# Another planned order for all engines of a sparse-attention and FFN kernel: new due-time shifts, new places for five copies

## The chip, the cores and the metric

The kernel runs on one core of a Trainium2 chip. Its time is the device time of one execution in microseconds (us); several executions give a median.

## What is computed

The reference is banded attention followed by a LayerNorm and a feed-forward network with a residual (4 batches, 8 heads, 768 positions, 64 columns a head; a query row sees the 8 first keys and the 96 last ones):

```python
scores = scale * np.matmul(q, k.transpose(0, 1, 3, 2)) + bias      # bias: -slope[h] * distance
scores = np.where(is_global | is_local, scores, -1000000000.0)
a = softmax(scores);  x = a @ v                                    # [4, 768, 8*64]
xn = (x - mu) / np.sqrt(var + 1e-06) * g_ln
out = x + np.maximum(xn @ w_ch1, 0.0) @ w_ch2                      # 512 -> 2048 -> 512
```

The weights arrive as 64-bit floats, the rest as 32-bit floats.

## The kernel before, in words

**Arithmetic.** Nearly every product is made of fp16 matmuls: each operand is split into a high and a low fp16 part, and three products (high by high, high by low, low by high) are summed in PSUM. So a "row" of probabilities times values is three matmuls at lines 512 to 514, a first-layer product three at 809 to 811, 837 to 839 or 862 to 864, and the second layer (line 910) reads `w2h`, `w2l`, `w2h`.

**Tiles and stages.** There are 24 tiles of 128 query rows, t0 to t23. t0 to t3 are the first blocks of the four batches; they run in fp32 at the start (flips of q and k by TensorE at 479 and 481, copies out of PSUM at 471 on ACT or 473 on DVE, scores at 583, the maximum at 593, exponentials at 597, product with v at 611, quotient at 621 to 623). A later tile runs group `.k` (load and split of k, q, v), `.s` (scores 685, least value 544 on DVE, exponentials 549 on ACT, high part 690 on DVE, low part 691 on POOL, transposing DMA, rows 512 to 514 on TensorE) and `.x` (quotient 524, moments 531 to 533, power 536 on POOL, normalization 708 on DVE and 718 on ACT, differences 726 to 729 on POOL, halves 740 on ACT and 741 on DVE, transposing DMA 742 into xT).

Two tiles make a chunk of 256 rows, f0 to f11 (tile 2c and 2c+1). f0 and f1 run the first layer in parts as soon as one tile is there (`a0` to `a3`), f2 and f3 directly, and f4 to f11 by `seven`: seven products of 24 matmuls (lines 862 to 864) for each half of the columns instead of eight, with copies (875, ACT), additions (878, DVE) and the eviction (820 ACT, then 821 DVE) between them, in three PSUM banks. Its first products per half take the first half of xT (`key` 0), the next ones sums and differences of the halves (made by 726 to 729, 740, 741). The second layer (910) takes 6 matmuls per step, and 919 with the DMA at 922 writes the result.

**Weights.** Sixteen weight blocks w0 to w15 of 1 MB are loaded (392) and turned into fp16 parts by passes a (400, ACT), b (404, DVE), c (412, ACT), d (416, DVE), the high part (435 POOL, 437 ACT) and the low part (439 POOL, 441 DVE). The letters of `WHERE` say which engine makes pass b, the high and the low part.

**What sets the order.** `banded` records every operation with engine, a planned duration and a group. `Plan.forward` then makes a list schedule: each operation has a due time from what needs it, moved by `SHIFT[group]`; of the operations that could start, an engine takes the most urgent one. An engine other than TensorE may stand idle for up to `LOOK` times the duration of that operation, if a more urgent one (by over `EAGER`) will be ready by then. `ORDER` gives the order in which groups stand in the rings of buffers, `MOVE` the engine of the copies at 471/473, `FLIPS` the PSUM banks for the flips of each first tile. The kernel then issues on each engine in exactly this order; every engine runs its list in order, so an operation that waits holds all behind it. `hold` (1022) puts matmuls on a constant into planned gaps of TensorE before 130 us; `tied` places a POOL operation behind the DVE operation that is planned ahead of it, before `TIED` = 150 us. The three tests of the inputs' ranges, `ranges` (972 to 977), `products` and `limits`, are DVE groups of their own.

Of the kernel before, what the change touches and what calls it, by code (L numbers as in the profile page):

```python
# [23 lines left out]
B, H, S, D = 4, 8, 768, 64  # L24
# [62 lines left out]
class Plan:  # L87
# [20 lines left out]
    def op(self, engine, took, emit, r=(), w=(), xfer=None, after=0.0, uses=(), port=False):  # L108
        o = Op(engine, took, emit, xfer, after, port)
        o.group = self.group  # L110
        for k in r:
            self.edges(self.wrote.get(k, ()), o)
        for k in w:
            self.edges(self.wrote.get(k, ()), o)
            self.edges(self.read.get(k, ()), o)
        for k in w:
            self.wrote[k], self.read[k] = [o], []
        for k in r:
            if k not in w:
# [21 lines left out]
    def order(self, chain, stretch, lead):  # L141
# [28 lines left out]
        self.need, self.place = need, place  # L170
        self.planned = self.forward(SHIFT)
        return [o for _, o in self.planned]

    def forward(self, shift):
# [18 lines left out]
        while any(known.values()):  # L193
            best = None
            for e in engines:
# [28 lines left out]
        return [(at, o) for at, _, o in sorted(plan, key=lambda x: x[:2])]  # L224


LOOK = 0.5
EAGER = 3.0


# [1 line left out]
def banded(ctx, tc, q, k, v, n_global, n_local, g_ln, w1, w2, out, flag):  # L232
# [155 lines left out]
    def weight(src, dh, dl, name, n, engine="SP", uses=()):  # L388
# [672 lines left out]
LAST = 40  # L1061
IDLE, HOLD, FILL = 3, 130.0, 0.8
CW = 4
ORDER = ["t01", "t23", "w0", "w1", "w2", "w3", "w4", "w5", "w6", "w7", "w8", "w9", "w10", "w11", "w12", "w13", "w14", "w15", *(f"a{t}{j}" for t in range(4) for j in range(4))]
FLIPS = {0: ("fl", (6, 7, 4)), 1: ("fl", (6, 7, 4)), 2: ("f2", (6, 7)), 3: ("f2", (6, 7))}
TS0 = list(range(12, 20))
LATER = (2, 3)
LOW_ON_POOL = ()
# [206 lines left out]
```

## Times and profile before

| | |
|---|---|
| median of 3 runs | 629.6 us (629.45, 629.6, 631.86) |
| the profiled execution's own time | 630.34 us |
| its span in the trace | 628.6 us |
| mean granted TensorE clock | 0.992 |
| TensorE busy | 602.3 us (96% of the span) |
| DVE, ACT, POOL busy | 442.3, 328.3, 246.0 us |

How to read it: the span is from the first to the last instruction in the trace; the time also holds the 1.7 us around it. Busy time counts from the start to the modelled end of an instruction; successive matmuls overlap, so the start-to-start distance and not the duration says how fast TensorE goes. A bracket behind a row, `[3.18 <-DVE arena L821]`, is the idle time of the engine ahead of this row and what ended it.

### The profile page before, as it was taken

The numbers are of one execution on the slowest core, as the hardware profiler recorded it, in microseconds if no ns is written. First come the engines' busy times: TensorE is split into PE (matmuls) and PEld (weight loads), VectorE is DVE, ScalarE is ACT, GpSimd is POOL, SyncE is SP. The second block draws the span as 40 slices with busy tenths as digits, with TensorE's granted clock in tenths as the row PEclk, the third lists the DMA queues.
The fourth block names the chain that finished last, engine by engine and source line by source line (L and its number), as shares of the span: only waits on it lengthen the run. The fifth ranks groups of instructions, "written<-read, shape, count | busy, mean of one in ns | idle before, by whom it ended". The sixth has DMA issues, their size and how long they took to land.

```text
span 628.6 us, 17087 instructions
## 1 busy us (share of the span) xinstructions
PE 602.3 (96%) x6988; PEld 450.9 (72%) x6988; DVE 442.3 (70%) x995; ACT 328.3 (52%) x798; POOL 246.0 (39%) x230
## 2 busy tenths in 40 slices
PE   7889999999999999799999999999899999999995
PEld 5778998545956866696786786786687695886762
DVE  3899898887648575885895994893785684773431
ACT  3887887654534454563663662671663562642220
POOL 1234354448774764432422532531533432422000
PEclk9999999999999999899999999999989999999999
DMA  9996989978484685897698896887996771641301
GB/s 241 304 281 137 247 219 245 169 157 188 76 151 86 142 144 119 173 184 115 133 163 165 167 160 134 165 122 140 169 170 107 157 136 35 126 69 19 77 1 39
DMA packets 260118, 91.64 MB, mean 146 GB/s; under 512 B 250176, under 2 KB 250176, under 8 KB 260032
## 3 DMA queue, kind: packets, MB, share of 16 engines
q1 hardware_dynamic: 259744, 90.47, 72.7%
q8 instruction: 56, 0.92, 0.6%
q14 instruction: 30, 0.25, 0.1%
q10 hardware_dynamic: 288, 0.00, 0.0%
HBM read 38.01 MB, written 6.29 MB: 70 GB/s over the span
## 4 chain that ended last, share of the span: by engine, by line
PE 68%; DVE 13%; ACT 5%; DMA 5%; POOL 4%; issue 3%; SPq 1%; ACTq 0%; DVEq 0%; POOLq 0%
PE bank L910 30%; PE bank L862 7%; PE bank L864 6%; PE bank L863 6%; PE bank L685 4%; PE bank L838 2%; PE bank L839 2%; PE bank L837 2%; DMA arena<-arena 2%; DVE arena L416 2%; DVE arena L404 2%; DMA arena<-in_moe_w_ch_dram 1%; ACT arena L549 1%; PE bank L514 1%; PE bank L512 1%
## 5 line engine op out<-in xcount | busy, mean ns | idle before, releaser
L910 PE MATMUL bank<-w2h,arena 128*128 128x512 f16 x768 | 245.6, 379 | 0.1
L910 PEld LDWEIGHTS <-arena 128*128 128x128 f16 x1152 | 107.2, 98 | 112.3 <-issue 0.9
L691 POOL TENSOR_TENSOR arena<-arena 128x512 f16<-128x512 f32 x80 | 95.6, 1197 | 169.4 <-DVE arena L690 111.6
L910 PE MATMUL bank<-w2l,arena 128*128 128x512 f16 x384 | 145.5, 379 | 0.1
L862 PE MATMUL bank<-arena 128*128 128x128 f16 x512 | 88.2, 219 | 2.8 <-DMA arena<-arena 1.7
L863 PE MATMUL bank<-arena 128*128 128x128 f16 x512 | 88.2, 219 | 0.0
L864 PE MATMUL bank<-arena 128*128 128x128 f16 x512 | 88.2, 219 | 0.0
L549 ACT ACTIVATE arena<-arena,mn 128x256 f32<-128x256 f32 x160 | 80.0, 501 | 5.1
L862 PE MATMUL bank<-arena,w 128*128 128x128 f16 x384 | 68.7, 223 | 3.2 <-DVE arena L821 3.2
L544 DVE CUSTOM_DVE_ANT_0 arena<-bank,mask 128x256 f32<-128x256 f32 x160 | 60.3, 418 | 13.7 <-POOL arena L691 9.8
L864 PE MATMUL bank<-arena,w 128*128 128x128 f16 x384 | 68.8, 223 | 0.0
L863 PE MATMUL bank<-arena,w 128*128 128x128 f16 x384 | 68.8, 223 | 0.0
L821 DVE SCALAR_TENSOR_TENSOR arena<-bank,arena 128x512 f16<-128x512 f32 x64 | 43.7, 686 | 26.3 <-ACT arena L820 25.7
L820 ACT ACTIVATE arena<-bank 128x512 f16<-128x512 f32 x64 | 37.7, 591 | 37.1 <-PE bank L864 34.0
L863 PEld LDWEIGHTS <-arena 128*128 128x128 f16 x512 | 50.2, 98 | 4.4 <-issue 3.3
L685 PE MATMUL bank<-kT,qT 128*128 128x128 f16 x640 | 47.0, 219 | 4.8 <-DVE nm L544 2.4
L862 PEld LDWEIGHTS <-arena 128*128 128x128 f16 x512 | 50.2, 98 | 0.9
L864 PEld LDWEIGHTS <-arena 128*128 128x128 f16 x512 | 50.1, 98 | 0.0
L536 POOL TENSOR_TENSOR rs<-rs,half 128x1 f32<-128x1 f32 x24 | 23.7, 987 | 65.9 <-DVE rs L533 65.9
L690 DVE CAST arena<-arena 128x512 f16<-128x512 f32 x80 | 41.6, 526 | 9.7 <-DMA arena<-arena 4.4
L685 PEld LDWEIGHTS <-qT 128*128 128x128 f16 x640 | 39.6, 98 | 12.0 <-issue 6.6
L547 ACT ACTIVATE mn<-nm 128x2 f32<-128x2 f32 x80 | 15.8, 197 | 56.2 <-DVE nm L544 55.6
(177 smaller groups left out, 1479.4 us busy)
## 6 DMA issues: line engine op xcount, KB each, us to landing
arena<-in_moe_w_ch_dram SPq DMA_DIRECT2D x16, 1024.0 KB, 7.4
kf<-in_k_dram SPq DMA_DIRECT2D x28, 256.0 KB, 4.4
vf<-in_v_dram SPq DMA_DIRECT2D x28, 256.0 KB, 4.0
qf<-in_q_dram SPq DMA_DIRECT2D x24, 256.0 KB, 3.8
out_dram<-x SPq DMA_DIRECT2D x24, 256.0 KB, 2.4
qT<-qT SPq DMA_DIRECT2D x40, 128.0 KB, 3.3
pT<-arena SPq DMA_TRANSPOSE x80, 3.5
arena<-arena SPq DMA_TRANSPOSE x36, 3.2
```

The costliest lines, as they stand in the source:

```text
L536: op("POOL", 0.98, lambda: pool.tensor_tensor(out=rs(), in0=rs(), in1=half, op=ALU.pow), r=["half"], w=[rs])
L544: vec.tensor_tensor_reduce(out=T()[:, u, :], in0=ps()[:, u], in1=mask(h), scale=1.0 / Z, scalar=3e38, op0=ALU.add, op1=ALU.min, accum_out= ...
L549: act.activation(out=T()[:, u, :], in_=T()[:, u, :], func=AF.Exp, scale=-1.0, bias=mn()[:, h:h + 1], accum_out=sm()[:, h:h + 1])
L685: pe.matmul(ps()[:, u, n_ * P:(n_ + 1) * P], lhsT=qT()[:, a * H + h, :], rhs=use[n_][0]()[:, h, :], start=(a == 0), stop=(a == 1))
L690: op("DVE", 0.33, lambda pn=pn, T=T: vec.tensor_copy(out=pn()[:, :, 0, :], in_=T()), r=[T], w=[(pn, "hi")], port=True)
L691: op("POOL", 1.2, lambda pn=pn, T=T: pool.tensor_tensor(out=pn()[:, :, 1, :], in0=T(), in1=pn()[:, :, 0, :], op=ALU.subtract), r=[T, (pn, ...
L820: op("ACT", 0.49, lambda: act.activation(out=hh()[:, 0], in_=src(), func=AF.Relu), r=[key], w=[(hh, "hi")])
L821: op("DVE", 0.6, lambda: vec.scalar_tensor_tensor(out=hh()[:, 1], in0=src(), scalar=0.0, in1=hh()[:, 0], op0=ALU.max, op1=ALU.subtract), r ...
L862: pe.matmul(ps()[:, i, :], lhsT=wh, rhs=xT()[:, hi + kk, :], start=(first_ and i == 0 and kk == 0), stop=False, skip_group_check=True)
L863: pe.matmul(ps()[:, i, :], lhsT=wh, rhs=xT()[:, lo + kk, :], start=False, stop=False, skip_group_check=True)
L864: pe.matmul(ps()[:, i, :], lhsT=wl, rhs=xT()[:, hi + kk, :], start=False, stop=(i == 3 and kk == 1), skip_group_check=True)
L910: pe.matmul(ps[t](), lhsT=h[:, part, :], rhs=w[:, f + a, :], start=(f + a == 0 and n_ == 0), stop=(f + a == NF - 1 and n_ == 2))
```

## The change

The numbers that set the order are replaced; no operation is added or dropped, and each operation keeps its shape. Of the passes over the weights, the high part of four blocks goes from ACT to POOL (before: ten on ACT, six on POOL; after: six and ten); eight low parts are on POOL in both. Six copies at 473 on DVE become five (one goes to ACT). The flips of t0 and t1 get a fourth PSUM bank, `t23` stands later in `ORDER`, and `LOOK` is doubled. The table `SHIFT` is another one in nearly every entry; here are its first ones.

```diff
-LOOK = 0.5
+LOOK = 1.0
...
-ORDER = ["t01", "t23", "w0", "w1", "w2", "w3", "w4", "w5", "w6", "w7", "w8",
+ORDER = ["t01", "w0", "w1", "w2", "w3", "w4", "w5", "w6", "w7", "t23", "w8",
...
-FLIPS = {0: ("fl", (6, 7, 4)), 1: ("fl", (6, 7, 4)), 2: ("f2", (6, 7)), 3: ("f2", (6, 7))}
+FLIPS = {0: ("fl", (6, 7, 4, 5)), 1: ("fl", (6, 7, 4, 5)), 2: ("f2", (6, 7)), 3: ("f2", (6, 7))}
...
-SHIFT = {"a0": 820.0, "a1": 286.0, "a2": 108.0, "a3": 701.5, "f0": 21.0, "f1": -345.5, "f10": -122.5,
...
+SHIFT = {"a0": 392.5, "a1": -70.0, "a3": 106.0, "f0": -21.0, "f1": 3.0, "f10": -16.5, "f2": -17.0,
...
-MOVE = {"k1": "D", "k3": "D", "p31": "D", "q0": "D", "q1": "D", "q3": "D"}
-WHERE = {"1_0_0": "DAP", "1_0_1": "DPP", "1_1_0": "DAD", "1_1_1": "DAD", "1_2_0": "DAD", "1_2_1": "DPD", "1_3_0": "DPD", "1_3_1": "DPP", "2_0": "DAP", "2_1": "DPP", "2_2": "DAP", "2_3": "DPD", "2_4": "DAP", "2_5": "DAD", "2_6": "DAD", "2_7": "DAP"}
+MOVE = {"k2": "D", "p01": "D", "p21": "D", "q0": "D", "q2": "D"}
+WHERE = {"1_0_0": "DPP", "1_0_1": "DAP", "1_1_0": "DPD", "1_1_1": "DAD", "1_2_0": "DPP", "1_2_1": "DPD", "1_3_0": "DPP", "1_3_1": "DAP", "2_0": "DPP", "2_1": "DPD", "2_2": "DPP", "2_3": "DAD", "2_4": "DPD", "2_5": "DPD", "2_6": "DAD", "2_7": "DAP"}
```

In the rows of the order that follow, `arena` is the large buffer in which most intermediate tiles lie, and a number behind a name tells its copies apart.

The first place is the start. These are the first operations of the ACT engine, ahead of them the loads of n_global and n_local, before the change:

```order
L377 ACT_TABLE_LOAD
L377 ACTIVATE arena<-arena,nh 128x256
L471 ACTIVATE k_0_198<-bank_78 128x512
L373 ACTIVATE mask_84<-arena 128x256 x8
L597 ACTIVATE arena<-bank_72,nm_250 128x128 x4
L471 ACTIVATE pT_0_281<-bank_79 128x512
```

and after it:

```order
L400 ACT_TABLE_LOAD
L400 ACTIVATE arena<-arena,less 128x1024
L412 ACTIVATE arena,big<-arena 128x1024
L400 ACTIVATE arena<-arena,less 128x1024
L437 ACTIVATE w_01_91<-arena 128x2x512
L412 ACTIVATE arena,big<-arena 128x1024
L377 ACTIVATE arena<-arena,nh 128x256
L471 ACTIVATE k_1_227<-bank_76 128x512
L471 ACTIVATE q_1_229<-bank_77 128x512
L373 ACTIVATE mask_84<-arena 128x256 x8
```

Five passes over the first two weight blocks now stand ahead of the mask (377, 373) and of the first copies of q and k. The same happened to the loads: on the SP queue the first weight block (392) went from behind five loads of q, k and v to the first place.

The second place is the quotient of tile t9 at about 250 us, where chunk f4 takes over. On DVE before:

```order
L919 SCALAR_TENSOR_TENSOR x_2777<-bank_79,x_2777 128x512
L690 CAST arena<-arena 128x2x256
L524 TENSOR_TENSOR x_3574<-bank_74,r_3281 128x512
L531 BN_STATS bn_3576<-x_3574 128x6
L532 BN_AGGR mv<-bn_3576 128x2
L533 TENSOR_SCALAR rs_3579<-mv 128x1
L708 SCALAR_TENSOR_TENSOR arena<-x_3574,mv,gb 128x512
L821 SCALAR_TENSOR_TENSOR arena<-bank_77,arena 128x512
L669 COPY vn_1_2775<-vn_0_2445 16x1024
```

and after:

```order
L690 CAST arena<-arena 128x2x256
L821 SCALAR_TENSOR_TENSOR arena<-bank_77,arena 128x512
L524 TENSOR_TENSOR x_3590<-bank_74,r_3289 128x512
L531 BN_STATS bn_3593<-x_3590 128x6
L532 BN_AGGR mv<-bn_3593 128x2
L533 TENSOR_SCALAR rs_3596<-mv 128x1
L708 SCALAR_TENSOR_TENSOR arena<-x_3590,mv,gb 128x512
L775 TENSOR_TENSOR arena<-arena 128x512
```

The eviction at 821, which frees bank_77, went from behind t9's five operations to the place ahead of them.

The third place is TensorE at the same point, between t9's last rows and the next product into bank_77. Before, the product stands right behind the rows:

```order
L514 LDWEIGHTS pT_3_3483
L514 MATMUL bank_74<-vn_1_2775,pT_3_3483 128x64
L862 LDWEIGHTS w_00_90
L862 MATMUL bank_77<-arena,w_00_90 128x128
L863 LDWEIGHTS w_00_90
```

After, six matmuls of f3's second layer (910) stand between them:

```order
L514 LDWEIGHTS pT_3_3478
L514 MATMUL bank_74<-vn_1_2782,pT_3_3478 128x64
L910 LDWEIGHTS arena
L910 MATMUL bank_79<-w2h,arena 128x512
L910 LDWEIGHTS arena
L910 MATMUL bank_79<-w2l,arena 128x512
```

and six more stand between the product before and the rows, so that twelve matmuls of the second layer and the twelve row matmuls are in between. Elsewhere in the program the same groups moved too: between the last rows of the second tile of a chunk and the first product that needs that tile's xT, the order now has other amounts of TensorE's work, which the prediction gives.

## Rows read from the trace of the kernel before

**Rows 1.** The page: busy us, share of the span and instructions of each engine.

```profile
PE 602.3 (96%) x6988; PEld 450.9 (72%) x6988; DVE 442.3 (70%) x995; ACT 328.3 (52%) x798; POOL 246.0 (39%) x230
```

**Rows 2.** Waits of TensorE from 130 us on: total us, times, longest.

```profile
PE bank L862 <- DVE arena L821: 3.2, 1, 3.2
PE bank L685 <- DVE nm L544: 2.3, 4, 1.4
PE bank L685 <- DVE kT L668: 2.2, 1, 2.2
PE bank L862 <- DMA arena<-arena: 1.7, 2, 1.1
PE bank L862 <- ACT bank L875: 1.0, 2, 0.7
```

**Rows 3.** Timeline of TensorE: start, duration, instruction, idle ahead of it.

```profile
250.84 0.19 PE L514 MATMUL bank<-vn,pT 128*128 128x64 f16 x1
254.21 0.27 PE L862 MATMUL bank<-arena,w 128*128 128x128 f16 x1 [3.18 <-DVE arena L821]
258.48 0.38 PE L910 MATMUL bank<-w2h,arena 128*128 128x512 f16 x1
258.69 0.38 PE L910 MATMUL bank<-w2l,arena 128*128 128x512 f16 x1
261.88 0.22 PE L862 MATMUL bank<-arena 128*128 128x128 f16 x1
402.33 0.22 PE L862 MATMUL bank<-arena 128*128 128x128 f16 x1 [1.10 <-DMA arena<-arena]
457.22 0.65 PE L685 MATMUL bank<-kT,qT 128*128 128x128 f16 x8 [2.22 <-DVE kT L668]
```

**Rows 4.** Timeline of ACT and DVE at 250 us.

```profile
250.72 0.60 ACT L820 ACTIVATE arena<-bank 128x512 f16<-128x512 f32 x1 [2.44 <-PE bank L864]
251.07 0.69 DVE L524 TENSOR_TENSOR x<-bank,r 128x512 f32<-128x512 f32 x1 [0.66 <-PE bank L514]
253.47 0.68 DVE L821 SCALAR_TENSOR_TENSOR arena<-bank,arena 128x512 f16<-128x512 f32 x1
```

**Rows 5.** Timeline of DVE at 455 us.

```profile
455.03 1.09 DVE L976 TENSOR_SCALAR okb<-big 128x16 f32<-128x16 f32 x1
```

**Rows 6.** Stretches: length, busy PE, PEld, DVE, ACT, POOL, granted clock, DMA share, GB/s.

```profile
253.50:256.90 3.40, 2.69 (x25) 2.66 (x25) 2.11 (x4) 1.27 (x2) 2.49 (x4) 0.50 0.94 201
458.30:461.70 3.40, 3.40 (x35) 3.27 (x33) 2.37 (x6) 2.47 (x10) 1.52 (x2) 0.50 0.79 162
```

**Rows 7.** The same columns, the start by tens.

```profile
0.00:10.00 10.00, 7.33 (x49) 5.54 (x49) 2.88 (x16) 2.77 (x5) 1.59 (x13) 1.00 0.83 162
10.00:20.00 10.00, 8.67 (x75) 7.47 (x75) 5.67 (x14) 7.33 (x20) 0.00 (x0) 1.00 1.04 379
20.00:30.00 10.00, 8.07 (x74) 7.21 (x71) 9.52 (x17) 8.65 (x18) 3.29 (x3) 1.00 1.02 283
```

**Rows 8.** Timeline of TensorE: the first fp32 scores.

```profile
11.32 1.16 PE L583 MATMUL bank<-k,q 64*128 64x128 f32 x8 [1.44 <-DVE q L473]
```

**Rows 9.** Groups of DVE and POOL by form: busy us, mean ns, idle before.

```profile
L404 DVE TENSOR_SCALAR arena<-arena 128x1024 uint16<-128x1024 uint16 x16 | 23.2, 1464 | 2.1 <-ACT arena L400 2.1
L416 DVE SCALAR_TENSOR_TENSOR arena<-arena 128x1024 int32<-128x1024 int32 x16 | 21.2, 1322 | 1.1 <-ACT arena L412 1.1
L435 POOL CAST w<-arena 128x1024 f16<-128x1024 f32 x3 | 3.4, 1137 | 9.5 <-DVE arena L416 7.2 <-DVE w L441 2.3
```

**Rows 10.** Timeline of DVE and POOL at 35 to 40 us.

```profile
35.01 1.22 DVE L416 SCALAR_TENSOR_TENSOR arena<-arena 128x1024 int32<-128x1024 int32 x1
37.35 1.30 DVE L404 TENSOR_SCALAR arena<-arena 128x1024 uint16<-128x1024 uint16 x1
38.80 2.13 POOL L439 TENSOR_TENSOR w<-arena,w 128x1024 f16<-128x1024 f32 x1 [1.37 <-DVE arena L404]
39.93 2.08 DVE L416 SCALAR_TENSOR_TENSOR arena<-arena 128x1024 int32<-128x1024 int32 x1 [0.23 <-ACT arena L412]
```

More of the change, by code (lines that the diff above doesn't have):

```diff
@@ L1063 @@
 CW = 4
-ORDER = ["t01", "t23", "w0", "w1", "w2", "w3", "w4", "w5", "w6", "w7", "w8", "w9", "w10", "w11", "w12", "w13", "w14", "w15", *(f"a{t}{j}" for t in range(4) for j in range(4))]
-FLIPS = {0: ("fl", (6, 7, 4)), 1: ("fl", (6, 7, 4)), 2: ("f2", (6, 7)), 3: ("f2", (6, 7))}
+ORDER = ["t01", "w0", "w1", "w2", "w3", "w4", "w5", "w6", "w7", "t23", "w8", "w9", "w10", "w11", "w12", "w13", "w14", "w15", *(f"a{t}{j}" for t in range(4) for j in range(4))]
+FLIPS = {0: ("fl", (6, 7, 4, 5)), 1: ("fl", (6, 7, 4, 5)), 2: ("f2", (6, 7)), 3: ("f2", (6, 7))}
 TS0 = list(range(12, 20))
@@ L1082 @@
 SS, PVS, PVS2, F1S, F1S2, F2S, F2S2 = (0, 1), (2, 3), (2,), (4, 5), (4, 5, 3), (6, 7), (6, 7)
-SHIFT = {"a0": 820.0, "a1": 286.0, "a2": 108.0, "a3": 701.5, "f0": 21.0, "f1": -345.5, "f10": -122.5, "f11": 112.5, "f2": 34.5, "f4": 18.0, "f5": -6.5, "f6": 9.5, "f7": -72.5, "f8": -87.5, "f9": 42.0, "g": 43.0, "m.a": 196.5, "m.d": -8.5, "s": 25.5, "t0.k": -12.0, "t0.p": 442.5, "t0.s": -26.0, "t0.x": 120.0, "t1.k": -11.0, "t1.p": 823.0, "t1.s": 740.5, "t1.x": 391.0, "t10.k": 4.5, "t10.s": 71.5, "t10.x": 151.5, "t11.k": -0.5, "t11.s": 51.0, "t11.x": 97.5, "t12.k": 162.0, "t12.s": 43.0, "t12.x": -52.5, "t13.k": -41.0, "t13.s": -78.5, "t13.x": 214.5, "t14.k": -152.5, "t14.s": -0.5, "t14.x": 327.5, "t15.k": -122.0, "t15.s": -30.0, "t15.x": -41.5, "t16.k": 49.5, "t16.s": 21.5, "t16.x": 22.0, "t17.k": -339.0, "t17.s": -103.0, "t17.x": -150.0, "t18.k": -10.5, "t18.s": 113.5, "t18.x": -59.5, "t19.k": 62.5, "t19.s": -44.5, "t19.x": 153.0, "t2.k": -612.5, "t2.p": 446.0, "t2.s": -18.0, "t2.x": 531.5, "t20.k": 147.0, "t20.s": 192.5, "t20.x": 207.0, "t21.k": -140.5, "t21.s": -33.0, "t21.x": 166.0, "t22.k": 85.0, "t22.s": 67.5, "t22.x": 76.0, "t23.k": -42.0, "t23.s": -129.0, "t23.x": 17.0, "t3.k": -590.0, "t3.p": 320.0, "t3.s": -371.0, "t3.x": 98.0, "t4.k": -338.0, "t4.s": 227.0, "t4.x": 59.0, "t5.k": 1576.5, "t5.s": 804.0, "t5.x": 1039.0, "t6.k": -664.5, "t6.s": 75.0, "t6.x": 87.5, "t7.k": 211.5, "t7.s": 189.5, "t7.x": 31.0, "t8.k": 61.5, "t8.s": -1.0, "t8.x": 1.5, "t9.k": -35.5, "t9.s": 13.0, "t9.x": 149.5, "w1_0_0": -19.0, "w1_0_1": -367.5, "w1_1_0": -7.5, "w1_1_1": -360.0, "w1_2_0": -44.5, "w1_2_1": -300.0, "w1_3_0": 297.0, "w1_3_1": 841.0, "w2_0": -334.5, "w2_1": 76.0, "w2_2": -332.0, "w2_3": 22.5, "w2_4": -548.0, "w2_5": -183.0, "w2_6": -33.5, "w2_7": 16.5}
@@ L1084 @@
-MOVE = {"k1": "D", "k3": "D", "p31": "D", "q0": "D", "q1": "D", "q3": "D"}
-WHERE = {"1_0_0": "DAP", "1_0_1": "DPP", "1_1_0": "DAD", "1_1_1": "DAD", "1_2_0": "DAD", "1_2_1": "DPD", "1_3_0": "DPD", "1_3_1": "DPP", "2_0": "DAP", "2_1": "DPP", "2_2": "DAP", "2_3": "DPD", "2_4": "DAP", "2_5": "DAD", "2_6": "DAD", "2_7": "DAP"}
+SHIFT = {"a0": 392.5, "a1": -70.0, "a3": 106.0, "f0": -21.0, "f1": 3.0, "f10": -16.5, "f2": -17.0, "f3": -11.5, "f4": -38.5, "f5": 2.5, "f6": 9.5, "f7": -19.5, "f8": -26.0, "f9": -37.0, "g": -252.0, "m.a": 158.5, "s": -24.5, "t0.p": 219.5, "t0.x": 237.0, "t1.k": 81.5, "t1.s": -621.5, "t1.x": 151.5, "t10.k": -29.5, "t10.s": 52.0, "t10.x": -6.0, "t11.k": 4.5, "t11.s": -44.0, "t12.k": 21.0, "t12.s": 39.0, "t12.x": 37.5, "t13.k": 32.5, "t13.s": 34.0, "t13.x": 21.5, "t14.k": -86.0, "t14.s": 33.0, "t14.x": 97.0, "t15.k": -61.5, "t15.s": 7.0, "t15.x": 116.5, "t16.k": 50.0, "t16.s": 45.5, "t17.k": -129.5, "t17.s": -12.0, "t17.x": 45.0, "t18.k": -116.5, "t18.s": 120.5, "t19.s": -43.0, "t19.x": 85.5, "t2.s": 350.5, "t20.s": 39.0, "t21.k": 23.5, "t21.s": -34.0, "t22.s": 156.5, "t23.k": 34.0, "t23.s": 51.5, "t3.k": 93.5, "t3.p": -7.5, "t3.x": -6.0, "t4.k": 25.0, "t4.s": 378.5, "t5.k": -151.5, "t5.s": -19.5, "t5.x": 89.0, "t6.k": 115.5, "t7.k": -106.5, "t7.s": -19.0, "t8.k": -106.0, "t8.s": -14.5, "t8.x": -28.5, "t9.k": -27.0, "t9.s": -10.5, "t9.x": 28.0, "w1_0_0": 340.5, "w1_0_1": 430.5, "w1_1_0": 2.5, "w1_1_1": -2.0, "w1_2_0": 54.5, "w1_2_1": 23.5, "w2_2": 3.0, "w2_3": 7.5, "w2_4": 285.5, "w2_5": -84.5, "w2_6": 190.5, "w2_7": 167.0}
```

## The prediction

> **What bounds the kernel now.** I read the page's busy times first, then the waits of TensorE, then the timeline at the longest of them, then the granted clock by stretches, and last the start by tens. TensorE is busy for 96% of the span and no other engine for over 70% [rows 1], so the end is set by TensorE's own work and by the time in which it stands idle, works on constants or runs at half its clock. No matmul that computes something is added or dropped, so only those three can change.
>
> From 130 us on, where no constants are fed in any more, five groups of waits make 3.2 + 2.3 + 2.2 + 1.7 + 1.0 = 10.4 us [rows 2]. The longest is one stop of 3.18 us at 254.21: a product of f4 wants bank_77, and the eviction at 821 has not freed it [rows 3]. The ACT half of that eviction started at 250.72 and took 0.60, so DVE could have gone on at 251.3; but its list had t9's quotient and moments (524 to 708) ahead, and 821 started at 253.47 [rows 4]. The second, 2.22 us at 457.22, comes from the copy of kT at 668 [rows 3], which stood on DVE behind the six small operations of `ranges`, one of which took 1.09 us [rows 5]. Behind each of these two stops TensorE is granted half its clock, 0.50 (the level of 1.2 GHz), for 3.4 us [rows 6]. In the first one TensorE stood until 254.21, so 2.7 us of work ran at half speed, which costs 1.3 us; in the second 3.4 us, which costs 1.7. That is 3.0 us for the clock. The other waits are short: transposed halves of xT that were late (1.10 at 402.33 [rows 3]), score banks, a copy.
>
> The start is another matter. In the first 20 us DVE is busy for 2.88 + 5.67 of 20 us, from 20 us on for 9.52 of 10 [rows 7]: it idles while the first q and k come in, and is then the engine that the rest waits for. TensorE's wait of 1.44 us ahead of its first fp32 scores at 11.32 is for a copy on DVE [rows 8].
>
> **The change part by part.** *f4's stop.* On DVE 821 now stands ahead of t9's quotient, and on TensorE six matmuls of f3's second layer stand on either side of t9's rows. At the distance of 0.21 us between two such matmuls [rows 3] that is 12 x 0.21 = 2.6 us, and the rows take 0.3 (2.9 us together); the eviction needs 0.60 + 0.68 = 1.3 us [rows 4]. So the 3.2 us go, with 1.6 us in hand. What hides the eviction is that second layer; without it 1.0 us of wait would remain. What is late next is t9's own chain, through quotient, power, normalization, differences, halves and transposing DMA, to the first product that needs xT.
>
> *The chunk boundaries.* That chain took at most 11.0 us at f4, from t9's last row at 250.84 to the first product that reads sums of xT at 261.88, which shows no wait [rows 3]. At f7 a product waited 1.10 us [rows 3], with 11.7 us of TensorE's work in the order between the rows and it, so there the chain took 12.8 us. I take 11.0 to 12.8. Counting, in the two orders, TensorE's work between those two points at the trace's distances between matmuls gives for f4 to f11: before 5.6, 11.6, 11.6, 11.7, 10.4, 14.2, 11.7, 12.9 us; after 9.5, 12.9, 14.2, 14.3, 14.7, 13.4, 14.7, 11.7. In the old order six of the eight lie under 12.8, in the new one two: f4, short by 1.5 to 3.3 us, and f11, by 0 to 1.1. At f4 the chain itself showed 11.0 with foreign work on DVE ahead of it, so I take 1.5 there, and 0.5 at f11. The waits for DMA and 875 (2.7) thus shrink to 2.0.
>
> *`ranges` and kT.* In the new order the tests stand where DVE has about 6 us until TensorE needs what follows, and kT's copy is not behind them: 2.2 us go. If that cover is gone, they come back. The score banks' waits (2.3 us, four times) have no one cause; the slack that I count behind their operations in the new order is smaller than zero in a few places, by 0.8 at most, where it was 4.6 before. I keep half, 1.1 (bounds 0 and 2.3). So of 10.4 us there remain 2.0 + 1.1 = 3.1: a gain of 7.3.
>
> *The clock.* The two dips stood behind idle times of 3.18 and 2.22 us. Behind the 1.10 at 402.33 none stood. The longest wait that I leave is 1.5, so I count none: a gain of 3.0 (bounds 0 and 3.0).
>
> *The start.* Five ACT passes and four DVE passes over two weight blocks, with 2 MB of loads between, move ahead of the mask and of the first copies of q and k. For DVE they are twice 1.30 + 1.22 [rows 10], 5.0 us, put into time in which it was idle for 11.5 us [rows 7]. Against that, everything of the first tiles comes later: stepped through by the durations of the trace the first fp32 scores start near 17.8 instead of 11.3 [rows 8], and a0's first group at 40.4 as before, but with 5.4 us less of TensorE's work done by then. DVE's idle time to that point grows by 3.0 by this count. On the other side the largest lead that TensorE has on DVE's list shrinks from 11.8 to 11.2 us, and it falls to 5 to 7 us after that, where it stayed at 8 to 10 in the old order; 2.2 us that TensorE lost between 70 and 130 us hang on this. 3.0 - 0.6 - 2.2 is 0.2: I count nothing. The bounds are -3 (the later waits go and DVE idles no longer) and +6 (the first scores' delay stays whole). The matmuls on constants rise from 154 to 188; where the planned gaps are not real, they are part of these +6. The fourth flip bank and the copy that goes to ACT cost 0 or less; they fall into DVE's busiest time and into the same bounds.
>
> *The four high parts.* ACT is relieved of four passes and does not bind. POOL takes four of 1.14 us [rows 9], in time in which it is idle for over half. But a DVE pass beside a POOL pass is held: 416 took 2.08 us at 39.93, while the low part at 439 ran from 38.80 to 40.93 on POOL, and 1.22 at 35.01 [rows 10]. Over all 16, 404 lost 16 x (1464 - 1300) ns and 416 16 x (1322 - 1220) [rows 9, 10], 2.6 + 1.6 us beside 14 POOL passes: 0.3 each. So four more cost 1.2 us; the bounds are 0 and 4 x 0.86 = 3.4, if each hits a pass as at 39.93. All of that falls where DVE binds.
>
> The Trainium skill, page "SBUF — State Buffer", section "SBUF: two separate sides", speaks against this part: VectorE and GpSimd share one pair of ports under a lock, and the one that comes later is blocked for the whole instruction. This trace agrees for 416, which ended about one duration behind POOL's pass. By that rule each of the four could cost a whole pass of 1.14, 4.6 us instead of 1.2, and the sum would end 3.4 us later. The rows' mean of 0.3 says that the ties keep most passes apart, and I stay with it.
>
> **The sum.** 630.3 - 7.3 - 3.0 + 0 + 1.2 = 621.2 us for an execution like the profiled one. That one lies 0.7 above the median, so 620.5 is my number. At 450 to 500 us, say, TensorE then has nothing left but work; the end of the program (the last result and its store behind the last matmul) does not move.
>
> **The rivals.** *The gain is eaten at the start.* DVE gets its first copy some 6 us later, its list keeps the lead it needs, and the +6 stays, less little: 620.5 + 6 to 8 (with the POOL passes at their bound) is 627 to 629, within 0.5%. For it speaks that DVE has 9.5 of 10 us busy right behind, so idle time before 20 us is never won back; against it that 5.0 us of that work now are done there.
>
> *f4's stop moves instead of going.* DVE's 821 stands behind 690 and 775 (a high part and a sum of weights), which wait for others; if one is late, or if t9's chain takes 12.8, TensorE stands for 3 us again, with a dip: 620.5 + 1.8 + 1.5 + 1, about 625, still faster.
>
> *Slower.* `LOOK` at 1.0 leaves more planned idle time on DVE, ACT and POOL in favour of urgent work. If that work comes later on the chip than planned, every chain from a tile's rows to xT grows. With 3 us more, a mean of 15 us, the eight boundaries are short by 5.5 + 2.1 + 0.8 + 0.7 + 0.3 + 1.6 + 0.3 + 3.3 = 14.6 us, and two of them (f4, f11) bring a dip of 1.7 each: 630.3 - 13.4 + 14.6 + 3.4, with the POOL passes 636, or about 635 by the median. It decides from chains of 14 us on. Against it speaks that the chains' operations and the foreign work ahead of 741 (0.4 to 3.2 us) are about the same in both orders.
>
> **How the numbers follow.** My forecast gets 0.60, the moved stop 0.14, the start 0.17, the slower case 0.09. About 0.5% (3.1 us) is what a measurement of this kernel can tell from no change, so faster means under 626.5 and slower over 632.8. Faster: 0.60 and 0.14, 0.74. Same: 0.17. Slower: 0.09. The range goes from 614 (waits left of 3.1 gone, -3 at the start, less the POOL cost) to 629 (the start's case), and leaves out the slower case and a little below.
>
> **What would show it.** Right: from 130 us on under 4 us of waits of TensorE, no wait for 821 at f4, none for kT, granted clock 1.00 in every stretch of 50 us, the sums' product of f4 1 to 3 us late; at 130 us as much work done as before; 404 and 416 with about the same means. Wrong: first fp32 scores near 18 us with no less work of DVE behind them and TensorE's waits before 70 us longer by several us (the start); waits for transposed halves at most boundaries (the slower case); 416 or 441 near 2 us in most rows (the port).

## The result: slower by 1%

The changed kernel takes 635.8 us (median of six runs, 635.2 to 636.8) against 629.5 us before: a ratio of 1.0099, with a 95% interval from 1.0079 to 1.0119. The forecast was 620.5 us, in a range up to 629. Its profiled execution has a span of 634.1 us, 5.5 us more than before. Some executions of the kernels here run 4 to 12 us longer at a lower granted clock; they are left out of every comparison, so that a median below is that of the others.

First the page's line of busy times and then the waits of TensorE of the changed kernel, from 130 us on (compare [rows 1] and [rows 2]; columns as there):

```profile
PE 609.6 (96%) x7022; PEld 456.3 (72%) x7022; DVE 447.2 (71%) x994; ACT 327.8 (52%) x795; POOL 254.6 (40%) x234
```

```profile
PE bank L685 <- DVE nm L544: 3.2, 2, 2.7
PE bank L862 <- DVE arena L878: 0.7, 1, 0.7
PE bank L910 <- DVE arena L821: 0.5, 1, 0.5
PE bank L685 <- DVE kT L668: 0.4, 1, 0.4
```

The middle came out much as it was meant: 10.4 us of waits became 4.8, the stop of 3.2 us for 821 and that of 2.2 us for kT are gone, and so are the waits for transposed halves. But in the first 130 us more is lost than the middle wins. The waits there, and then the stretches of the start (columns as in [rows 6, 7]):

```profile
PE bank L481 <- DMA kf<-in_k_dram: 3.6, 1, 3.6
PE bank L1022 <- DVE x L623: 2.7, 1, 2.7
PE bank L587 <- DVE arena L369: 1.8, 1, 1.8
PE bank L583 <- ACT q L471: 1.1, 2, 0.6
```

```profile
0.00:10.00 10.00, 7.41 (x45) 5.54 (x45) 0.77 (x5) 2.44 (x2) 1.66 (x13) 1.00 0.59 211
10.00:20.00 10.00, 7.51 (x50) 6.26 (x51) 7.41 (x9) 6.17 (x10) 3.48 (x3) 0.83 1.26 278
20.00:30.00 10.00, 8.04 (x55) 6.12 (x53) 6.47 (x15) 6.92 (x19) 2.02 (x1) 0.83 0.86 230
40.00:50.00 10.00, 7.90 (x59) 6.23 (x59) 4.58 (x13) 2.27 (x4) 2.22 (x3) 0.66 0.97 228
```

TensorE's busy time hides the loss, since matmuls on constants count as busy. So I counted useful work: each matmul of the computation is worth its usual distance to the next one (0.056 us for 128 columns, 0.216 for 512), and what a stretch is longer than that sum is lost. Up to 130 us the old trace loses 34.3 us and the new one 46.2, 11.9 more (8.8 of it before 50 us, 3.6 from 50 to 90); behind 130 us the old one loses 14.6 and the new one 8.3, 6.3 less. 11.9 - 6.3 is 5.6, the whole difference of the spans; the tail behind the last matmul is the same to 0.1 us. (The expectations below were written with 7.0 for the 6.3.)

DVE shows the same loss. In the first 70 us it was busy for 55.9 us before and for 45.5 now (lines of the first 70 us, before and then after): it idles for 10.4 us more. One wait alone is 5.2 us of that, for the copy at 465 behind the 25 matmuls on constants (below).

```profile
0.00:70.00 70.00, 61.17 (x640) 53.51 (x641) 55.88 (x98) 51.73 (x96) 20.45 (x28) 1.00 0.91 240
```

```profile
0.00:70.00 70.00, 57.90 (x501) 48.35 (x502) 45.48 (x75) 43.40 (x81) 15.53 (x25) 0.90 0.75 202
```

### Three places in the new trace

*The first loads.* The rows that answer to [rows 8]: flips and first fp32 scores on TensorE. The first k lands behind the weight blocks, at 12 us (the first flip was at 6.50 before), and the first scores start at 17.82 instead of 11.32.

```profile
12.00 0.63 PE L481 MATMUL bank<-arena,kf 128*128 128x128 f32 x4 [3.59 <-DMA kf<-in_k_dram]
17.82 1.16 PE L583 MATMUL bank<-k,q 64*128 64x128 f32 x8 [0.49 <-ACT q L471]
```

*The mask.* DVE's passes over the second weight block and the mask, and POOL's passes beside them:

```profile
16.44 2.08 DVE L416 SCALAR_TENSOR_TENSOR arena<-arena 128x1024 int32<-128x1024 int32 x1 [1.30 <-ACT arena L412]
18.89 1.16 DVE L363 TENSOR_TENSOR arena<-arena 128x256 f32<-128x256 f32 x1
20.08 2.08 DVE L364 SCALAR_TENSOR_TENSOR arena<-arena,cnt 128x128 f32<-128x128 f32 x1
```

```profile
15.29 2.14 POOL L439 TENSOR_TENSOR w<-arena,w 128x1024 f16<-128x1024 f32 x1 [12.99 <-DVE arena L404]
18.58 1.18 POOL L435 CAST w<-arena 128x1024 f16<-128x1024 f32 x1 [1.15 <-DVE arena L416]
19.84 2.17 POOL L439 TENSOR_TENSOR w<-arena,w 128x1024 f16<-128x1024 f32 x1
```

364 took 0.35 us in the old trace and 363 took 0.42. Here each of the three ends behind the POOL pass at its side, by 1.09, 0.29 and 0.15 us, at most its own free duration: 363 began at 18.89, POOL's pass ended at 19.76, and 363 ended at 20.05. The ties keep a POOL pass from starting inside the DVE pass planned ahead of it; they don't cover the mask's passes, which are not marked for it.

*The 25 matmuls on constants.* TensorE and ACT at t0's normalized rows:

```profile
42.05 5.16 PE L1022 MATMUL bank<-still 128*128 128x252 bf16 x25 [2.69 <-DVE x L623]
47.05 0.60 PE L481 MATMUL bank<-arena 128*128 128x128 f32 x4
```

```profile
41.70 0.72 ACT L637 ACTIVATE arena<-arena,rs 128x512 f32<-128x512 f32 x1 [0.99 <-POOL rs L536]
```

The flips at 481 had their input at 42.42. But the constants, planned for the gap ahead of it, write the PSUM bank that the quotient at 623 still reads; so they did not fill it. TensorE stood for 2.69 us, and then ran them at 0.2 us each: the granted clock from 42.05 to 47.2 us was 0.54. The first products of a0 (809) behind them, in the old trace and then in the new one:

```profile
40.85 0.23 PE L809 MATMUL bank<-arena,w 128*128 128x128 f16 x1
```

```profile
48.80 0.22 PE L809 MATMUL bank<-arena,w 128*128 128x128 f16 x1
```

### The profile page after: what moved, and what is told of

Read it like the earlier page. It is cut to its first block, busy times and chain, and to the rows that moved or that the text cites. A ratio compares the mean times of both kernels' runs of the same rounds, so it can differ in the third digit from the quotient of the medians.

```text
span 634.1 us, 17178 instructions
## 1 busy us (share of the span) xinstructions
PE 609.6 (96%) x7022; PEld 456.3 (72%) x7022; DVE 447.2 (71%) x994; ACT 327.8 (52%) x795; POOL 254.6 (40%) x234
## 4 chain that ended last, share of the span: by engine, by line
PE 72%; DVE 12%; DMA 6%; ACT 5%; issue 2%; POOL 1%; SPq 1%; ACTq 0%; DVEq 0%; POOLq 0%
PE bank L910 30%; PE bank L862 7%; PE bank L863 7%; PE bank L864 7%; PE bank L685 5%; DMA arena<-in_moe_w_ch_dram 4%; DVE arena L404 2%; PE bank L839 2%; PE bank L837 2%; PE bank L838 2%; DVE arena L416 1%; PE bank L512 1%; PE bank L514 1%; PE bank L1022 1%; PE bank L513 1%
## 5 line engine op out<-in xcount | busy, mean ns | idle before, releaser
L691 POOL TENSOR_TENSOR arena<-arena 128x512 f16<-128x512 f32 x80 | 97.5, 1221 | 155.9 <-DVE arena L690 123.0
L862 PE MATMUL bank<-arena,w 128*128 128x128 f16 x384 | 66.8, 219 | 0.7 <-DVE arena L878 0.7
L864 PE MATMUL bank<-arena,w 128*128 128x128 f16 x384 | 66.8, 219 | 0.0
L863 PE MATMUL bank<-arena,w 128*128 128x128 f16 x384 | 66.8, 219 | 0.0
L536 POOL TENSOR_TENSOR rs<-rs,half 128x1 f32<-128x1 f32 x24 | 25.6, 1067 | 60.7 <-DVE rs L533 60.7
L690 DVE CAST arena<-arena 128x512 f16<-128x512 f32 x80 | 40.1, 509 | 6.8 <-DMA arena<-arena 3.6
```

The costliest lines, as they stand in the source:

```text
L536: op("POOL", 0.98, lambda: pool.tensor_tensor(out=rs(), in0=rs(), in1=half, op=ALU.pow), r=["half"], w=[rs])
L690: op("DVE", 0.33, lambda pn=pn, T=T: vec.tensor_copy(out=pn()[:, :, 0, :], in_=T()), r=[T], w=[(pn, "hi")], port=True)
L691: op("POOL", 1.2, lambda pn=pn, T=T: pool.tensor_tensor(out=pn()[:, :, 1, :], in0=T(), in1=pn()[:, :, 0, :], op=ALU.subtract), r=[T, (pn, ...
L862: pe.matmul(ps()[:, i, :], lhsT=wh, rhs=xT()[:, hi + kk, :], start=(first_ and i == 0 and kk == 0), stop=False, skip_group_check=True)
L863: pe.matmul(ps()[:, i, :], lhsT=wh, rhs=xT()[:, lo + kk, :], start=False, stop=False, skip_group_check=True)
L864: pe.matmul(ps()[:, i, :], lhsT=wl, rhs=xT()[:, hi + kk, :], start=False, stop=(i == 3 and kk == 1), skip_group_check=True)
```

## The experiments

All orders are written out as lists, so that an edit moves what it names and nothing else is planned anew; a name like `t0.x:7` is the seventh operation of group t0.x. `LOOK`, `MOVE`, `FLIPS` and `ORDER` were not tried alone. `LOOK` acts only through the order that was planned with it; `ORDER`, `MOVE` and `FLIPS` also say which buffers, engines and banks are used, and go with the kernel that gives the start. Median times are against 629.5 to 630 us of the kernel before on the same chip.

### Which half is it? Old and new orders put together

```diff
+early = [(at_, o) for at_, o in plan.planned if at_ < 130.0]
+plan.planned = early + [(130.0, named[k_]) for k_ in REST]
...
```

(225 stands for 130 in the third run.) `REST` holds all other operations in the other kernel's order; engines and constants are those of the kernel that gives the start.

> The operations planned before 130 us in the kernel before its change keep that kernel's order, engines and matmuls on constants; all later ones follow the changed kernel's order. Theory A (two separate halves: the new start loses 11.9 us up to 130 us, the new order behind it wins 7.0): about 622.5 us (621 to 625), with under 1 us of waits for 821 and kT. Rival B (the middle only looks better because TensorE arrives there 12 us later, so that all other engines have more in hand): about 629, with the old waits at chunk boundaries back.

Measured: two runs, 623.3 and 625.3 us (too few for an interval). Theory A holds, B falls: the middle gains with an early TensorE as well.

> The mirror image: the changed kernel's order, engines and matmuls on constants before 130 us, the old order behind. Theory A: 629.5 + 11.9 = 641 us (639 to 643), the start of the changed kernel's trace and the waits of the old middle. Rival B: the old middle loses less when TensorE comes later, 630 to 636.

Measured: 645.6 us, ratio 1.0243 (1.0222 to 1.0264); four of the five runs lie at 643.9 to 645.7, the profiled one at 651.7. The old middle's stops came back (3.2 us for 821, 1.4 for kT). The new start costs 14 to 16 us with the old middle and 11.9 with the new one, over the range of theory A (639 to 643). Rival B is out; what it costs more with the old middle fits a wait at the seam, 2.7 us for transposed probabilities at 151 us, which was not tested.

> The kernel before up to the operations planned at 225 us, the changed kernel's order behind. Behind 250 us the old trace loses 14.6 us against the pace of its matmuls, the changed one 7.1, and the run with the new order from 130 us on lost 3.5 there. Theory A: 629.5 - 14.6 + 3.5 to 7.1, 618.5 to 622 us. Rival B (the new middle needs the new way up to it): waits at f4 and behind the seam like in the old one, 625 to 630.

Measured: 622.5 us, ratio 0.9877 (0.9846 to 0.9908). With the cut behind the stretch in which the old kernel ran without a loss, the gain is over 7 us, the time 0.5 us above theory A's range, and one stop at a chunk boundary is left, at f4 (below).

### The constants

```diff
+n = 0 if key[o] in ('t0.x:7',) else n
```

> The changed kernel without the 25 matmuls on constants that stand ahead of the flips of t0's normalized rows (at 42.05 us in its trace; they took 5.16 us at half clock, while the flips' input was there at 42.4). Nothing else is changed. Theory A (these matmuls stand in the way): the flips start at about 42.5 instead of 47.05, and the end comes 3 to 4.6 us earlier, 631 to 633 us. Rival C (the start is set by the weight blocks and DVE's list, so TensorE would only wait a little later): 635 to 636.

Measured: 630.6 us (seven runs, 630.4 to 632.1), 5.2 less than the changed kernel. The flips start at 42.01 instead of 47.05, while the products with v ahead of them start at 36.90 instead of 37.37:

```profile
42.01 1.09 PE L481 MATMUL bank<-arena 128*128 128x128 f32 x4 [3.11 <-ACT arena L637]
```

So these 25 matmuls cost what they took; theory A holds, 0.6 us beyond its 4.6, and rival C is out.

### POOL beside the mask

```diff
+later(("w1_0_1:7", "w1_0_0:6", "w1_0_0:7"), "m.a:4")
+named["m.a:4"].port = True
```

> The changed kernel with three POOL passes over the first two weight blocks (439, 435, 439) issued behind the last mask pass on DVE (369) instead of beside the mask passes. Theory A (POOL holds DVE): 363 and 364 take about 0.4 us each instead of 1.16 and 2.08, 416 1.2 instead of 2.08, the mask is ready some 3.3 us earlier, and the end comes 2 to 3.3 us earlier, 632.5 to 634 us. Rival C (weights and DVE's later list set the start): the mask is earlier, the time stays at 635 to 636.

This run is a miss of mine. The load that reuses the first block's place (`w1_3_0:1`) stayed ahead of the moved passes, so POOL converted that block after it was overwritten, and waited for the load until 33.2 us. Its 641.3 us say nothing on the edit; only its first 24 us do, and there the mask's last pass ended at 20.1. The next run moves the load as well:

```diff
+later(("w1_0_1:7", "w1_0_0:6", "w1_0_0:7", "w1_3_0:1"), "m.a:4")
```

> The changed kernel with the three POOL passes over the first two weight blocks behind the last mask pass on DVE, and with the load that reuses the first block's place behind them too (in the run before, that load had stood ahead of the passes). Theory A (POOL holds DVE beside the mask passes, and the mask is on the path): the mask's last pass ends near 20.1 us instead of 23.4, and the end comes 2 to 3.3 us earlier, 632.5 to 634 us. Rival C (the weights set the start): 635 to 636.

Measured: 631.4 us, 4.4 less than the changed kernel, ratio 1.0028 (1.0010 to 1.0046). DVE at the same place:

```profile
16.46 1.23 DVE L416 SCALAR_TENSOR_TENSOR arena<-arena 128x1024 int32<-128x1024 int32 x1 [1.29 <-ACT arena L412]
18.05 0.43 DVE L363 TENSOR_TENSOR arena<-arena 128x256 f32<-128x256 f32 x1
18.51 0.35 DVE L364 SCALAR_TENSOR_TENSOR arena<-arena,cnt 128x128 f32<-128x128 f32 x1
```

The mask is ready 3.3 us earlier, as theory A said, and the end comes 4.4 us earlier, 1.1 more than its bound (by the spans of the profiled executions 3.4). Rival C is out.

> Both edits: the POOL passes behind the mask, and no 25 matmuls on constants ahead of t0's flips. Theory A (two separate losses on one path): 4 to 5 us from the one and 2 to 3.3 from the other, 627.5 to 629.5 us. Rival C: the second removes what the first already gave, 630.5 to 632.

Measured: 628.5 us, 7.3 less than the changed kernel, ratio 0.9976 (0.9958 to 0.9994). Theory A holds by the time, and rival C is out; but alone the edits gave 5.2 and 4.4 us, so 2.3 of these 9.6 were the same time. The first products of a0 now start 6.1 us earlier than in the changed kernel:

```profile
42.72 0.31 PE L809 MATMUL bank<-arena,w 128*128 128x128 f16 x1
```

What remains of the start is the difference to the runs with the old start: 628.5 - 624.3, about 4 us, against the cut at 130 us, and 6 to 7 against the cuts at 225 (622.5) and at 90 us (621.8, below). The count of useful work agrees with the larger figure: up to 130 us this run still loses 41.5 us, 7.1 more than the kernel before, 3.5 of it before 50 us and 4.4 from 50 to 90.

### The rest of the start's loss

```diff
+sooner(("t1.k:1", "t1.k:2"), "w1_0_1:1")
...
+sooner(("t1.k:5", "t1.k:6", "t1.k:7", "t1.k:8"), "w1_0_0:2")
```

The left-out lines move the mask passes in the same way, and 30 and 24 matmuls on constants are set ahead of the first flips and scores (24 ahead of the scores in the next run, too).

> As the run with both edits, and the first loads of k and q, their copies and the mask passes put ahead of the first weight block's later passes and of the second block. Theory A (what is left of the lost 11.9 us is that weights stand ahead of q, k and mask): first fp32 scores near 14 us instead of 17.8, end at 623.5 to 626 us. Rival C (the early weights were needed so early; now a0's first products wait for them): 627.5 to 629.5, with TensorE's wait moved from the first scores to 811 or 809.

Measured: 633.2 us, 4.7 more than without this edit. The loads of k and q took the first weight block's time on the DMA engines: it landed at 11.21 instead of 7.55, the copies of k and q stand behind its passes on ACT, and the scores still start at 17.31:

```profile
11.21 1.28 ACT L400 ACT_TABLE_LOAD   x1 [11.21 <-DMA arena<-in_moe_w_ch_dram]
```

```profile
17.31 2.07 PE L583 MATMUL bank<-k,q 64*128 64x128 f32 x8 [6.92 <-ACT q L471]
```

So it did not make the scores early, and says nothing on them. Weights that come 3.7 us later go with an end 4.7 us later here; since TensorE also stood for 6.92 us ahead of the scores, what the weights' delay costs by itself is not shown.

> As the run with both edits of the start (POOL passes behind the mask, no 25 matmuls), with the first k and q loads between the first and the second weight block instead of behind both, their copies on ACT ahead of the second block's passes, and the mask ahead of 416. The first weight block keeps the first place, since with k and q ahead of it it landed 3.7 us later. Theory A (what is left of the loss is the late first scores): first fp32 scores near 13.7 us instead of 17.8, 624 to 626 us. Rival C (a0 and DVE's list wait for the weights in any case): first scores early, 627.5 to 629.5 us.

Measured: 628.5 us (six runs, 628.0 to 629.3). The first scores did start at 14.23, but the next ones, of the other tile, only at 21.23 (22.11 without the edit). The rows are of its profiled execution (633.9 us; granted clock 1.00 up to 20 us):

```profile
14.23 1.16 PE L583 MATMUL bank<-k,q 64*128 64x128 f32 x8 [0.97 <-ACT q L471]
21.23 1.16 PE L583 MATMUL bank<-k,q 64*128 64x128 f32 x8 [1.86 <-ACT k L471]
```

Rival C's number came: the first scores were 3.6 us earlier, and the end came no earlier than 628.5. The late first scores, on which the prediction's bound rested, are not by themselves what the rest hangs on; the scores behind them came only 0.9 us earlier, so late q and k as a whole are not ruled out.

> The kernel before with its own order in every place, but the high parts of the weights on the engines of the changed kernel (seven from ACT to POOL, three from POOL to ACT; low parts as they were). The predicted price of the four more POOL passes was 1.2 us with bounds 0 and 3.4: 629.5 to 633, likeliest 630.7 us. If POOL's hold on DVE is worse than the mean of 0.3 us for a pass: above 633.

Measured: 634.5 us, ratio 1.0076 (1.0061 to 1.0092), 5 us more, and over the upper bound. But the passes 404 and 416 are together only 1.0 us longer than before (16 of each, with means of 1538 and 1308 ns, 1464 and 1322 in [rows 9]). Most of the cost stands beside new waits of the old order for a POOL that is now late: 2.7 us of TensorE for a low part at 439, and 1.9 us for flips behind ACT. I read it as the price of new engines in an order made for others.

> The changed kernel with both edits of the start (POOL passes behind the mask, no 25 matmuls; 628.5 us), its order kept, but the high parts of the weight blocks from the third on back on the engines of the kernel before (six from POOL to ACT, two from ACT to POOL). Theory E (the added POOL passes are the rest of the loss): 3 to 5 us less, 623.5 to 625.5 us. Rival F (the rest lies in the order: weights ahead of q and k, and DVE's list): 627.5 to 629.5 us, or more where ACT now comes late.

Measured: 629.5 us, ratio 0.9988 (0.9973 to 1.0003). Theory E falls: with the copies from the third block on back on ACT the new order is no faster. The engines of these high parts aren't the rest of the loss.

> The kernel before (its own order, engines and matmuls on constants) for all that it planned before 50 us, the changed kernel's order behind, without matmuls on constants there. With the cut at 130 us it was 624 us, with the changed start 635.8, with the changed start and two edits 628.5. Theory G (the loss arises in the first 50 us, by DVE waiting for weights and copies there): 622 to 626 us. Rival H (the part that the two edits don't give back arises between 50 and 130 us): 627 to 630 us.

Measured: 628.2 us, ratio 0.9963 (0.9940 to 0.9986). The number is rival H's, but the trace has a stop at the seam that the changed kernel has not, so it can't tell:

```profile
60.16 0.29 PE L809 MATMUL bank<-arena,w 128*128 128x128 f16 x1 [4.60 <-POOL w L435]
```

> The same with the cut at 90 us. Theory G: 622 to 626 us, like the cuts at 50 and 130. Rival H: between the cut at 50 and the cut at 130, 624 to 628 us.

Measured: 621.8 us, ratio 0.9869 (0.9824 to 0.9914), like the cuts at 130 and 225. So with the old order up to 90 us the loss is gone: it arises from what the new order does before that. For the part that the two edits leave, the cause stays open. What goes with it: even with both edits DVE is busy for only 47.3 of the first 70 us (55.9 in the old order), and its passes over the first weight blocks wait for ACT's in turn, 404 for 400 and 416 for 412, for 7.1 us against 1.1 before. That this is the cause is argued, not shown, and three rivals stand untested. One is the clock: over the first 70 us the mean granted clock is 0.93 with both edits and 1.00 in the old start; behind the wait of 3.11 us for t0's rows 12 matmuls on constants took 2.73 us, in the changed kernel 1.47. One is the other matmuls on constants: from 50 to 90 us there are 35, in the old start 15. And one is the new banks and copy engines (`FLIPS`, `MOVE`).

### f4's stop: POOL and the halves

The stop that was left in the new middle is no longer for 821. In the changed kernel TensorE, then DVE, then POOL, and then the stretch behind the stop:

```profile
271.64 1.17 PE L685 MATMUL bank<-kT,qT 128*128 128x128 f16 x11 [2.65 <-DVE nm L544]
```

```profile
266.80 1.23 DVE L741 TENSOR_TENSOR arena<-arena 128x512 f16<-128x512 f32 x1 [1.41 <-ACT arena L740]
267.96 0.68 DVE L919 SCALAR_TENSOR_TENSOR x<-bank,x 128x512 f32<-128x512 f32 x1
268.56 2.34 DVE L741 TENSOR_TENSOR arena<-arena 128x512 f16<-128x512 f32 x2
```

```profile
266.75 0.73 POOL L729 TENSOR_TENSOR arena<-arena 128x256 f32<-128x256 f32 x1
267.44 1.62 POOL L761 TENSOR_TENSOR arena<-w,arena 128x512 f32<-128x512 f16 x1
269.14 1.48 POOL L761 TENSOR_TENSOR arena<-arena,w 128x512 f32<-128x512 f32 x1
```

```profile
272.00:275.40 3.40, 3.40 (x35) 3.22 (x33) 2.50 (x10) 3.34 (x14) 1.16 (x1) 0.51 0.46 126
```

The score bank is freed by 544, which stands on DVE behind t9's halves (741). The first half is held by POOL's last difference (729), the other two by its sums of weights (761); a dip to half clock follows, as behind the old stops. POOL is held in turn: its two sums take 1.62 and 1.48 us here, and 1.16 each where no half meets them (below). In the old trace the three halves took 2.16 us together:

```profile
257.01 2.16 DVE L741 TENSOR_TENSOR arena<-arena 128x512 f16<-128x512 f32 x3 [1.40 <-ACT arena L740]
```

In the run with the cut at 225 us, a tie goes from the last half (`t9.x:18`) to the first of the sums behind it (`s:64`).

```diff
+if key[o] in ("t9.x:18", "s:64"):
...
+    tc.add_manual_dep(new[0], ahead.pop(), SYNC, reason="port")
```

> The run with the old order up to 225 us and the new one behind, with one more dependency: POOL's sum of weights (761) that ran beside t9's halves on DVE (741) at 254 us waits for the last of these halves. Theory A (POOL's passes hold DVE, which is why f4's stop moved to the score bank behind the halves): the three 741 take about 0.69, 0.69 and 0.42 us instead of 1.23, 1.17 and 1.17, TensorE's wait for 544 at 255.4 falls from 2.6 to about 1.1 us and the stretch at half clock behind it goes: 618.5 to 620.5 us. Rival D (the halves' length is not POOL's doing, or the sums are then late): the wait stays at 2 us or more, or turns up at f4's later products; 621 to 623.

Measured: 619.1 us (three runs, 618.1 to 619.8), 3.4 less than without the tie; ratio 0.978 (0.965 to 0.991). Theory A holds by the time. Its first half is not freed: that one stands beside 729, which has no tie here, and in the next run, with the same tie, the first two halves together take 1.82 us.

> As the run with the dependency, and on DVE the first least value of t10's third pair of heads (544) goes ahead of the last half (741) and of f3's result (919). Theory A (what stands ahead of 544 in DVE's list makes the rest of the wait): another 1.1 us less, under 0.5 us of wait at 255 us, 617.5 to 619.5 us. Rival D: as the run with the dependency alone.

Measured: 620.9 us, ratio 0.980 (0.970 to 0.990): 1.8 more than with the tie alone. The wait for 544 at f4 came in two pieces of 0.5 and 1.0 us, and one of 0.9 us for a copy (875) joined it. Neither theory: the edit split the wait and added one.

```diff
-TIED = 150.0
+TIED = 1000.0
```

> The run with the old order up to 225 us and the new one behind (622.4 us), with the ties of POOL's passes to DVE's passes not ended at 150 us but kept to the end. If POOL's hold on DVE costs only at f4, as the single tie there (619 us): 618.5 to 620. If it costs at several places: below 618. If the ties make POOL late (each pass waits for the DVE pass planned ahead of it): 621 or more, with TensorE's waits on sums of weights or on rows 512.

Measured: 618.3 us (618.1 to 619.0), ratio 0.982 (0.980 to 0.984): the fastest of all, 11.3 us less than the kernel before on the same chip and 17.5 less than the changed kernel. Its rows show TensorE's wait at f4 (the granted clock in the 3.4 us from its end on is 1.00), t9's first half, POOL's first sum behind the halves, and the group of all 741 of this form:

```profile
256.40 1.29 PE L685 MATMUL bank<-kT,qT 128*128 128x128 f16 x16 [1.04 <-DVE nm L544]
```

```profile
253.18 0.69 DVE L741 TENSOR_TENSOR arena<-arena 128x512 f16<-128x512 f32 x1 [1.41 <-ACT arena L740]
```

```profile
255.74 1.16 POOL L761 TENSOR_TENSOR arena<-w,arena 128x512 f32<-128x512 f16 x1 [0.99 <-DVE arena L741]
```

```profile
L741 DVE TENSOR_TENSOR arena<-arena 128x512 f16<-128x512 f32 x24 | 17.1, 713 | 16.1 <-ACT arena L740 16.0
```

Without the ties that group had a mean of 925 ns. The time lies between the first two cases of the expectation. The single tie at f4 gave 3.4 of the 4.2 us; the others cost nothing, and the 0.8 us that they add are within the spread of the run with the single tie.

## Why the prediction was wrong, point by point

*The stops for 821 and kT, and the waits for transposed halves*: right. All are gone; the boundaries' cover, counted from the order, was the right measure.

*f4's remainder and the score banks*: mis-sized. I left 1.5 us at f4 for late halves, 1.1 for all score banks (2.3 at most) and no dip. No wait for a half is left, but the score banks took 3.2 us, 2.65 of it at f4 behind the halves, plus a dip. The chain that I took over from the old trace had the three halves in 2.16 us; beside POOL's passes they took 1.23 + 2.34. The rival in which f4's stop moves came true in its size, not in its cause (821, or a late xT). So the middle's 10.3 us (7.3 + 3.0) became 6.3.

*The start*: the step that failed. "3.0 - 0.6 - 2.2 is 0.2: I count nothing" was 11.9 us. The first scores at 17.8 were stepped right (17.82), but not what follows. I put a0's first products at 40.4 us; they started at 48.8 (40.85 in the old trace). Two things were in the text, at too small a size or in the wrong place. The matmuls on constants stood in a bound ("where the planned gaps are not real"), and cost 5.2 us: I had not seen that they use the bank that the quotient still reads, so that they can't fill the very gap they were planned for. And POOL's hold was priced as a mean over all passes, 0.3 us for each, when what counts is which DVE pass stands beside it: at the mask three passes met three, on the path, and cost 4.4 us. Both together are 7.3 us; for the rest of the 11.9 no run shows the cause.

*The four high parts*: the term of 1.2 us was asked of the wrong passes. Seven of them went to POOL and three came back, and from the third block on that is worth nothing in the new order (628.5 us with the new engines, 629.5 with the old ones); what cost was the place of two low parts and one high part, beside the mask.

The Trainium skill, page "SBUF — State Buffer", section "SBUF: two separate sides", has the sentence that I weighed and set aside: VectorE and GpSimd have a pair of ports under an exclusive lock, a VectorE instruction with two SBUF inputs takes it against a GpSimd one that reads SBUF, and whichever starts later is fully blocked. At the mask and at f4, where the passes are of this kind, the trace agrees (2.08 us for 0.35, 1.23 for 0.69, and POOL's 1.62 for 1.16). My mean of 0.3 us for a pass hid this.

*The rivals*: "the gain is eaten at the start" named the place, at 6 to 8 us where it was 11.9, so it stood on the side of no change; its reason, DVE's late first copy, is not what the runs showed. The slower case that I named (longer chains at all boundaries) did not happen: no wait for a transposed half is left. The range was too narrow because the start's upper bound of 6 us held only the first scores' delay, and moving those scores alone gave nothing.

## What to carry to other kernels

Price a shared port by the pair of instructions that meet on the path, not by the mean over all passes, and look for the passes that a guard leaves out. Work that fills planned gaps must not depend on what ends the gap. When a reordering changes a start and a middle, cut the two orders together at one point: here that turned a loss of 1% into a gain of 1.2%, and with POOL tied to DVE to the end into one of 1.8%.

## What was not expected of the hardware

A second pass on POOL right behind the first held DVE twice in a row: 363 (0.42 us alone) and 364 (0.35 us alone) took 1.16 + 2.08 = 3.24 us. And 0.5 MB of k and q rows ahead of a 1 MB weight block moved its landing by 3.7 us, from 7.55 to 11.21, about half of the time in which the block lands without them.
